# A spectral mixer with a token MLP on one core: a fixed engine order in the front, fixed PSUM banks and halved end units in the middle

## The chip, the cores and the metric

One NeuronCore of a Trainium2 chip runs the whole program. Its engines are TensorE (PE, with weight loads shown apart as PEld), VectorE (DVE), ScalarE (ACT), GpSimd (POOL) and SyncE (SP), which issues most of the DMAs. They run side by side, each takes its own instructions in the order in which they were written, and they wait for one another by semaphores. The metric is the time of one execution on the device, in microseconds (us).

## The reference

Two blocks, one after the other, on a sequence of 2048 tokens of 512 values, in bf16:

```python
def _A_ref(x, w_r, w_i):                 # x: 1 x 2048 x 512
    X = rfft2(x.astype(float32))         # over tokens and values: 2048 x 257 complex
    X = X * (w_r + 1j * w_i)             # one complex weight per frequency
    return irfft2(X, s=(S, D)).astype(bfloat16)

def _B_ref(x, w1, b1, w2, b2):           # mixes tokens: S = 2048, F = 1376
    h = _layernorm(x)
    u = gelu(einsum("bsd,sf->bdf", h, w1) + b1)
    return (einsum("bdf,fs->bds", u, w2) + b2).transpose(0, 2, 1)

h  = x + _A_ref(_layernorm(x), A_w_r, A_w_i)
h2 = h + _B_ref(_layernorm(h), B_w1, B_b1, B_w2, B_b2)
```

## The kernel before

The tokens are split as 128 partitions times 16 (n2), so x is sixteen tiles of 128 x 512. The Fourier transforms are written as matrix products with constant cosine and sine matrices, in five small stages, and the MLP as two large products.

1. **Front.** For each tile n2 the mean and the variance are found, on VectorE with `bn_stats` and `bn_aggr` (named st and ag, L653 and L654) or, for the tiles in `STAT_ACT`, on ScalarE with two passes and accumulators (s1, s2, L638) and two tiny steps on GpSimd (nm, bv). ScalarE turns the variance into 1/sigma (rs, L643 and L655; tiles of one entry of `RS_GROUPS` share one instruction). The 1/sigma of a tile scales its slice of the first Fourier matrix FP into FS (fs, on the engine that `FS_ENG` names, GpSimd otherwise). PE multiplies FS with the tile (f1: four matmuls of 256 columns per tile) into PSUM, and ScalarE, or VectorE for those in `Y_DVE`, copies the result to Y. One PSUM bank holds two tiles of one half b; there are sixteen copies of 512 elements.
2. **f2 and x.** The second transform works on Y of all sixteen tiles: for each of 16 values of G, four matmuls (f2), a copy to CS (cs; ScalarE, and VectorE for G = 1), and eight small matmuls (x) that fill two PSUM banks for two G's. Two G's make a unit u; there are eight.
3. **The multiply V (L739).** VectorE multiplies the PSUM of a unit with the filter weights W: one instruction of 2048 elements per unit, or two of 1024 where the unit is in `V_SPLIT`, here the first and the last.
4. **g1, g2, g3, the inverse transform.** g1 (16 matmuls per unit) is copied to PQ by ScalarE (pq, 512 elements for half a unit). g2 needs PQ of all units; its results are copied to EO, and g3 gives the filter block's output tile by tile. VectorE adds x (TT, H), ScalarE and VectorE normalise again (HH).
5. **The MLP.** 176 matmuls with W1 (mm1), gelu on ScalarE into GT, 176 with W2 (mm2), the last addition on VectorE, and the stores.

Nothing of this order is written out by hand. The class `Builder` collects the operations with their dependences, and `schedule` (L281) places them one at a time: of all operations that are ready it takes the one with the earliest planned start and, among equal starts, the one with the highest priority (`prio`), then the lowest index. The planned start uses a cost for each operation (`occ`: how long the engine is taken; `lat`: when the result is there) and a model of the DMA rate. The order in which operations are placed is the order of the instructions of each engine. PSUM units (`PsumUnit`) get banks at that moment: the bank, or neighbouring pair, that is free the earliest, with a limit on open units per class (f1 6, f2 2, x 2, g1 2).

At the start PE runs twenty matmuls on a tile of zeros (`warm`, L620 to L625; priority 50, while f1 has 14), which begin when VectorE's memset of that tile is done, and later some more behind the f1 matmuls (`WARM_AFTER`, priority 13) and ahead of the last half unit of g1 (`G1_WARM`).

The loads: x comes in six pieces and the FP constants in four; two of FP are issued by ScalarE, all else by SP. The filter weights W come in three pieces of units (0, 1 to 3, 4 to 7). A piece takes four DMAs for each of the two weight tensors, and the first piece six, because the row of partition `4 * (k2 * 2 + s) + 2 * sign + comp` (L37) interleaves the two signs of the frequency.

Of the kernel before, what the change touches and what calls it, by code (L numbers as in the profile page):

```python
# [6 lines left out]
ACT = mybir.ActivationFunctionType  # L7
# [29 lines left out]
def _row(sign, comp, k2, s):  # L37
    return 4 * (k2 * 2 + s) + 2 * sign + comp
# [52 lines left out]
def build_consts():  # L91
# [22 lines left out]
    fp = fp.reshape(NP, NS2, NP)  # L114
    fp = np.stack([-fp, fp], axis=2)
# [26 lines left out]
    c["E"] = e.reshape(NP, 1024)  # L142
    c["MR"] = np.concatenate([m.reshape(NP, 512), r.reshape(NP, 512)], axis=1)
# [5 lines left out]
PSUM_BANKS = 8  # L149
CELL = 4  # L150
# [28 lines left out]
class Builder:  # L179
    def __init__(self, nc, limits):  # L180
        self.nc = nc
        self.ops = []
        self.writer = {}
        self.readers = {}
        self.tensors = {}
        self.limits = limits
        self.cell_cache = {}

# [37 lines left out]
    def op(self, name, engine, emit, ins=(), outs=(), occ=100.0, lat=None, unit=None, pr=False, pw=False,  # L226
           first=False, last=False, prio=0, nbytes=0, is_dma=False, not_before=0.0, after=(), group=None, rate=DMA_RATE):
# [13 lines left out]
        o.rate = rate  # L241
        deps = {id(d): d for d in after}
# [38 lines left out]
    def schedule(self):  # L281
# [13 lines left out]
        order = []  # L295
        while len(order) < len(ops):
            best = None
            for o in ready:
                bank, avail = None, 0.0
                u = o.unit  # L300
                if u is not None and not u.claimed:
# [5 lines left out]
                    for b in range(PSUM_BANKS - u.nbanks + 1):  # L307
                        if all(bank_unit[i] is None for i in range(b, b + u.nbanks)):
# [13 lines left out]
            ready.remove(o)  # L322
            o.sched, o.start = True, st
# [11 lines left out]
            if o.is_dma:  # L335
                x0 = max(st + (3200.0 if st < 4000.0 else 1700.0), dma_free)
                dma_free = x0 + o.bytes / o.rate
# [89 lines left out]
def memory_layout():  # L427
# [26 lines left out]
    add("W", [NP, NG, 2, LW], bf, rw)  # L454
    add("HH", [NP, NS2, D_LEN], bf, rw)
# [28 lines left out]
STAT_ACT = (1, 3)  # L484
RS_GROUPS = ((0,), (2,), (4,), (5,), (6, 7), (8, 9), (10, 11), (12,), (13,), (14,), (15,))
FS_ENG = {4: "act", 7: "act", 9: "dve", 11: "dve", 13: "dve", 14: "act", 15: "dve"}
Y_DVE = ((5, 1), (6, 1), (7, 1))
N_WARM = 20
WARM_AFTER = (4, 3, 2, 1, 1, 0, 1, 0, 0, 0, 0, 0, 0, 0, 0, 0)
V_SPLIT = (0, 7)  # L490
# [4 lines left out]
def build_kernel(nc, A_x, A_w_r, A_w_i, B_w1, B_b1, B_w2, B_b2, out):  # L495
# [5 lines left out]
    K = Builder(nc, {"f1": 6, "f2": 2, "x": 2, "g1": 2, "g2": 2, "g3": 2, "mm1": 5, "mm1b": 6, "mm2": 8})  # L501
# [3 lines left out]
    X, FS, Y, CS, V, PQ, EO, H, HH, GT, OUT, W = (T[n] for n in ("X", "FS", "Y", "CS", "V", "PQ", "EO", "H", "HH", "GT", "OUT", "W"))  # L505
# [9 lines left out]
    def dma(name, dst, src, nbytes, stream="sp", outs=(), ins=(), prio=0, strided=False, after=(), group=None, rate=DMA_RATE,  # L515
            not_before=0.0):
        def emit(eng, bank):
            if strided:
                with nc.allow_non_contiguous_dma(reason="small bias gather"):
# [3 lines left out]
                    rate=rate, occ=1000.0 if stream == "pool" else 640.0 if rate < DMA_RATE else 460.0, not_before=not_before)  # L523
# [10 lines left out]
    def act(name, dst, src, func, n, ins=(), outs=None, unit=None, prio=0, last=True, psum=True, bias=None, scale=None, accum=None):  # L534
# [15 lines left out]
        return K.op(name, "act", emit, ins=ii, outs=oo, occ=lat - 90.0, lat=lat + 50.0, unit=unit, pr=unit is not None,  # L550
# [13 lines left out]
    def ldf(q, pr_, stream="sp", nb=0.0):  # L564
        sl = slice(4 * q, 4 * q + 4)
        dma(f"ld_FP{q}", FP[:, sl, :, :], cin[f"FP{q}"][:, :, :, :], 1 << 18, outs=[FP[:, sl, :, :]], prio=pr_, stream=stream, not_before=nb)

    for q, (a, b) in enumerate(((0, 2), (2, 4), (4, 6), (6, 8), (8, 12))):
        ldx(a, b, 90 - q)
    ldf(2, 84)  # L570
    ldx(12, 16, 83)
    ldf(3, 82)
    ldf(0, 90, "act")
    act("table", T["tb"][:, 0:1], EPS[:, 0:1], ACT.Abs_reciprocal_sqrt, 1, ins=[EPS[:, 0:1]], prio=88)
    ldf(1, 87, "act", 1800.0)
    dma("ld_E", EM[:, 0:1024], cin["E"][:, :], 1 << 18, outs=[EM[:, 0:1024]], prio=44)
    dma("ld_MR", EM[:, 1024:2048], cin["MR"][:, :], 1 << 18, outs=[EM[:, 1024:2048]], prio=43)
    wload = {}
    for ch, (u0, u1) in enumerate(((0, 1), (1, 4), (4, 8))):
        g0, ng = 4 * u0, 4 * (u1 - u0)  # L580
        lst = []
        for w, dram in ((0, A_w_r), (1, A_w_i)):
            for comp in range(2):
                d = W[comp::4, g0:g0 + ng, w, :]
# [296 lines left out]
```

## Time and profile before

| | us |
|---|---|
| median of 8 runs (lowest, highest) | 134.12 (133.69, 134.67) |
| profiled execution | 133.8 |
| its span, first to last instruction | 132.3 |
| PE busy, of the span | 124.8 (94%) |
| VectorE busy | 69.3 (52%) |
| ScalarE busy | 63.3 (48%) |
| GpSimd busy | 12.4 (9%) |
| granted TensorE clock, mean | 0.996 |

Stages by the timeline: the front from 4.8 (first tile there) to 18.8 (last copy to Y); f2 and x until the first multiply at 21.4; the multiplies until 39.3; g1, PQ and g2 until 42.5; the H stage until about 68; the rest of the MLP to the end. In a row of the timeline the first number is the start, the second how long the group lasted, then come engine, line of the kernel, operation, output and inputs, how many there were, and in brackets how long the engine had been idle and who ended that. In the chain of waits each row is a stretch of the path that ended last.

### The profile page before, as it was taken

How to read it: one execution, taken by the hardware profiler on the slowest of the kernel's cores; microseconds unless marked ns; L12 is line 12 of the kernel's file. 1: busy time of each engine (PE TensorE's matmuls, PEld its weight loads, DVE VectorE, ACT ScalarE, POOL GpSimd, SP SyncE). 2: the span in 40 equal slices, each digit the busy share in tenths (PEclk: the TensorE clock that was granted, in tenths of full speed). 3: DMA queues.
4: the chain of work that ended last, by engine and by line, in shares of the span. 5: the costliest groups of instructions: out<-in, count | busy, mean ns of one | idle time of the engine just before them, and what ended most of it. 6: DMA issues, size and time to landing. Idle time of an engine off the chain costs nothing.

```text
span 132.3 us, 2023 instructions
## 1 busy us (share of the span) xinstructions
PE 124.8 (94%) x786; PEld 74.6 (56%) x786; DVE 69.3 (52%) x127; ACT 63.3 (48%) x146; POOL 12.4 (9%) x33
## 2 busy tenths in 40 slices
PE   6999989999987979999999999999999999999990
PEld 2436656788666736544434444456666666666660
DVE  0499867999981999999960000000242332423322
ACT  4579976978966999976689322222000000000000
POOL 0299920000300000000000000000000000000000
PEclk9999999999999999999999999999999999999998
DMA  4999699999999999992000000000112112111121
GB/s 118 336 405 363 149 260 275 300 301 284 406 423 424 414 402 413 416 297 71 0 0 0 0 0 0 5 0 0 40 40 73 46 40 82 42 59 60 40 79 40
DMA packets 16648, 22.16 MB, mean 168 GB/s; under 512 B 2720, under 2 KB 12960, under 8 KB 16128
## 3 DMA queue, kind: packets, MB, share of 16 engines
q1 hardware_dynamic: 16352, 21.52, 47.6%
q10 hardware_dynamic: 288, 0.52, 1.3%
q8 instruction: 6, 0.10, 0.3%
q14 instruction: 2, 0.02, 0.0%
HBM read 19.95 MB, written 2.10 MB: 167 GB/s over the span
## 4 chain that ended last, share of the span: by engine, by line
PE 51%; DVE 32%; ACT 9%; DMA 3%; POOL 2%; issue 1%; DVEq 0%; ACTq 0%
PE ps L531 51%; DVE V L739 13%; DVE H L799 7%; ACT Y L549 5%; DVE TT L790 4%; DVE TT L792 4%; DVE HH L804 4%; DMA X<-in_A_x_dram 3%; POOL FS L633 1%; ACT rs L549 1%; ACT FS L549 1%; ACT JK L549 1%; DVE OUT L829 1%; PE ps L621 0%; ACT PQ L549 0%
## 5 line engine op out<-in xcount | busy, mean ns | idle before, releaser
L531 PE MATMUL ps<-HH,W 128*128 128x512 bf16 (+1 forms) x176 | 40.7, 379 | 1.2 <-DVE HH L804 0.9
L531 PE MATMUL ps<-GT,W 128*128 128x512 bf16 (+1 forms) x176 | 38.2, 379 | 0.0
L829 DVE SCALAR_TENSOR_TENSOR OUT<-ps,B2f,H 128x512 bf16<-128x512 f32 x16 | 12.0, 751 | 48.7 <-PE ps L531 48.7
L531 PEld LDWEIGHTS ps<-GT,W 128*128 128x128 bf16 (+1 forms) x176 | 25.3, 144 | 12.8
L531 PEld LDWEIGHTS ps<-HH,W 128*128 128x128 bf16 (+1 forms) x176 | 17.2, 100 | 21.3 <-DVE HH L804 1.9
L739 DVE TENSOR_TENSOR V<-ps,W 128x2048 bf16<-128x2048 f32 (+1 forms) x10 | 17.9, 1856 | 0.9 <-PE ps L531 0.9
L549 ACT ACTIVATE GT<-ps,B1f 128x512 bf16<-128x512 f32 (+1 forms) x11 | 7.1, 688 | 14.6 <-PE ps L531 14.6
L549 ACT ACTIVATE JK<-H,nm 128x512 bf16<-128x512 bf16 x16 | 11.6, 724 | 3.0 <-DVE H L799 2.9
L621 PE MATMUL ps<-ZT 128*128 128x512 bf16 x34 | 10.4, 445 | 1.3 <-DVE ZT L617 1.2
L653 DVE BATCH_NORM_STATS2 st<-X 128x6 f32<-128x512 bf16 x14 | 9.3, 671 | 4.0 <-DMA X<-in_A_x_dram 4.0
L799 DVE TENSOR_TENSOR H<-ps,TT 128x512 bf16<-128x512 f32 x16 | 11.0, 687 | 0.0
L549 ACT ACTIVATE PQ<-ps 128x512 bf16<-128x512 f32 x16 | 8.9, 603 | 3.5 <-PE ps L531 3.3
L549 ACT ACTIVATE EO<-ps 128x512 bf16<-128x512 f32 x16 | 9.2, 598 | 0.9 <-PE ps L531 0.9
L531 PE MATMUL ps<-EM,V 128*128 128x128 bf16 x128 | 9.2, 220 | 0.5 <-DVE V L739 0.5
L531 PE MATMUL ps<-EM,PQ 128*128 128x256 bf16 x64 | 9.0, 273 | 0.7 <-ACT PQ L549 0.7
L549 ACT ACTIVATE CS<-ps 128x512 bf16<-128x512 f32 x15 | 8.3, 608 | 2.1 <-PE ps L531 2.1
L531 PE MATMUL ps<-EM,Y 128*128 128x256 bf16 x64 | 8.7, 273 | 0.4 <-ACT Y L549 0.4
L531 PEld LDWEIGHTS ps<-EM,V 128*128 128x128 bf16 x128 | 7.5, 98 | 2.3 <-issue 1.4
L633 POOL TENSOR_SCALAR FS<-FP,rs 128x256 bf16<-128x256 bf16 x9 | 8.6, 962 | 0.6 <-ACT rs L549 0.5
L531 PE MATMUL ps<-FS,X 128*128 128x256 bf16 x64 | 8.4, 274 | 0.1
L790 DVE TENSOR_TENSOR TT<-ps,X 128x256 f32<-128x256 f32 x16 | 6.7, 421 | 3.3 <-PE ps L531 3.3
L531 PEld LDWEIGHTS ps<-EM,PQ 128*128 128x128 bf16 x64 | 6.2, 98 | 2.9 <-ACT PQ L549 0.9
(36 smaller groups left out, 79.7 us busy)
## 6 DMA issues: line engine op xcount, KB each, us to landing
W<-in_B_w_dram SPq DMA_DIRECT2D x4, 1376.0 KB, 12.0
W<-in_B_w_dram SPq DMA_DIRECT2D x10, 512.0 KB, 17.6
out_dram<-OUT SPq DMA_DIRECT2D x16, 128.0 KB, 1.7
W<-in_A_w_r_dram SPq DMA_DIRECT2D x4, 257.0 KB, 4.6
W<-in_A_w_i_dram SPq DMA_DIRECT2D x4, 257.0 KB, 4.7
X<-in_A_x_dram SPq DMA_DIRECT2D x4, 256.0 KB, 5.0
X<-in_A_x_dram SPq DMA_DIRECT2D x2, 512.0 KB, 6.7
W<-in_A_w_r_dram SPq DMA_DIRECT2D x4, 192.8 KB, 3.3
```

Of the source, the lines that this page charges most:

```text
L531: return K.op(name, "pe", lambda eng, bank: eng.matmul(outf(bank), lhsT, rhs, start=start, stop=stop), ins=ins or [lhsT, rhs], occ=occ, la ...
L549: return eng.activation(dst, s, func, **kw)
L621: return K.op(name, "pe", lambda eng, bank: eng.matmul(ps[:, bank, :], ZT[:, 0:NP], ZT[:, :], start=True, stop=True), ins=[ZT[:, :]], occ= ...
L633: dve(f"fs{i}", lambda eng, bank: eng.tensor_scalar(FS[:, i, :, :], FP[:, i, :, :], rs, None, op0=ALU.mult), [FP[:, i, :, :], rs], [FS[:, ...
L653: dve(f"st_{i}", lambda eng, bank, i=i, x=x: eng.bn_stats(ST[:, i, 0:6], x), [x], [ST[:, i, 0:6]], 512, prio=25)
L739: return eng.tensor_tensor(vout, s, win, ALU.mult)
L790: dve(f"tl_{s2}", lambda eng, bank, tt=tt, xl=xl: eng.tensor_tensor(tt[:, 0, :], ps[:, bank, 256:512], xl, ALU.add), [xl], [tt[:, 0, :]], ...
L792: dve(f"th_{s2}", lambda eng, bank, tt=tt, xh=xh: eng.tensor_tensor(tt[:, 1, :], xh, ps[:, bank, 256:512], ALU.subtract), [xh], [tt[:, 1, ...
L799: return eng.tensor_tensor(hs.rearrange("p (h d) -> p h d", h=2), e, tt[:, :, :], ALU.add)
L804: dve(f"hh_{s2}", lambda eng, bank, s2=s2, hs=hs: eng.tensor_scalar(HH[:, s2, :], hs, NM[:, s2:s2 + 1], R2[:, s2:s2 + 1], op0=ALU.add, op1 ...
L829: dve(f"fin{s2}", lambda eng, bank, dst=dst, bia=bia, hs=hs: eng.scalar_tensor_tensor(dst, ps[:, bank, :], bia, hs, op0=ALU.add, op1=ALU.add),
```

## The change

- The order of the front's operations is given by lists for VectorE, ScalarE, GpSimd and PE (`FRONT`). `schedule` takes an operation that is in a list only when all before it in the same list have been placed. Operations that are in no list, the fillers for example, are placed as before.
- The statistics of tiles 3 and 7 (before: 1 and 3) are found by ScalarE, from sums instead of means, so that one tiny GpSimd step (bv) lies on the way; nm moves behind the front. The FP slices of these tiles are scaled by 512 for it. The groups of rs and the engines of fs and of the copies to Y change. f1 fills a bank with one tile, both halves, or two neighbouring banks with two tiles; a copy to Y takes 512, 1024 or 256 elements, and VectorE does more of them.
- The first X piece of two tiles becomes two. ScalarE's two FP loads wait for the memset of zeros. Two loads of constants (E, MR) become one.
- The filter's rows are reordered (sign and comp swap) and the first filter piece gets a tile of its own, W0, weight tensor outermost, with eight DMAs instead of twelve.
- f2 and g1 use PSUM banks 0 to 3 only, x the pairs 4-5 and 6-7. f1 may have seven units open.
- Unit 0: each G's f2 result is copied in two halves, one by ScalarE, one by VectorE; each G's x has a unit of its own; the multiply is four instructions of 512 elements. Only unit 7 stays in `V_SPLIT`.
- The last half unit of g1 takes two banks, and its copy to PQ is two of 256 elements, the first by VectorE, the second by ScalarE.
- In the planner's costs a ScalarE operation takes the engine 30 ns less, and a DMA starts 1750 ns after its issue at 340 bytes/ns at first.

```diff
-    return 4 * (k2 * 2 + s) + 2 * sign + comp
+    return 4 * (k2 * 2 + s) + 2 * comp + sign
...
+    for i in STAT_ACT:
+        fp[:, i] *= D_LEN
...
+CLASS_BANKS = {"x": (4, 6), "f2": (0, 1, 2, 3), "g1": (0, 1, 2, 3)}
...
+        pos = {n: (e, i) for e, lst in self.forced.items() for i, n in enumerate(lst)}
+        done = {e: 0 for e in self.forced}
         while len(order) < len(ops):
             best = None
             for o in ready:
+                if o.name in pos and done[pos[o.name][0]] != pos[o.name][1]:
+                    continue
...
-                        if all(bank_unit[i] is None for i in range(b, b + u.nbanks)):
+                        if b in CLASS_BANKS.get(u.cls, range(8)) and all(bank_unit[i] is None for i in range(b, b + u.nbanks)):
...
-STAT_ACT = (1, 3)
-RS_GROUPS = ((0,), (2,), (4,), (5,), (6, 7), (8, 9), (10, 11), (12,), (13,), (14,), (15,))
-FS_ENG = {4: "act", 7: "act", 9: "dve", 11: "dve", 13: "dve", 14: "act", 15: "dve"}
-Y_DVE = ((5, 1), (6, 1), (7, 1))
+STAT_ACT = (3, 7)
+RS_GROUPS = ((0,), (1,), (2,), (4,), (5, 6), (8, 9), (10, 11), (12,), (13,), (14, 15))
+FS_ENG = {0: 'dve', 6: 'act', 7: 'act', 9: 'act', 10: 'dve', 15: 'dve'}
+Y_EVAC = (('single', ('dve',), ('act',)), ('pair', 'act'), ('pair', 'act'), ('pair', 'act'), ('single', ('act',), ('dve',)), ('pair', 'dve'), ('single', ('act',), ('act',)), ('single', ('dve', 'act'), ('act',)))
+FRONT = {
+    "dve": """bn_0 ag_0 fs_0 bn_1 ag_1 ys_0 bn_2 bn_4 ag_4 ag_2 bn_5 bn_6 ag_5 ag_6 bn_8 bn_9 ag_8 bn_10 ag_9 bn_13 ag_10
+        ag_13 bn_11 ag_11 bn_12 fs_10 ag_12 bn_14 bn_15 ag_14 ag_15 ys_9 fs_15 yp_5 yh_140""",
+    "act": """rs_0 rs_1 s1_3 s2_3 rs_3 ys_1 rs_2 rs_4 s1_7 rs_5 s2_7 fs_6 yp_1 rs_8 rs_7 fs_9 rs_13 fs_7 rs_10 yp_2 rs_12
+        yp_3 rs_14 ys_8 ys_13 ys_12 ys_15 yh_141""",
+    "pool": """fs_1 bv_3 fs_3 fs_2 fs_4 bv_7 fs_5 fs_8 fs_13 fs_11 fs_12 fs_14""",
+    "pe": """f1_0 f1_1 f1_3 f1_2 f1_4 f1_6 f1_5 f1_9 f1_8 f1_7 f1_10 f1_11 f1_13 f1_12 f1_15 f1_14""",
+}
-V_SPLIT = (0, 7)
+V_SPLIT = (7,)
...
     def stage_f2(u):
         for i in range(2):
             G = 2 * u + i
-            unit = PsumUnit("f2", 1)
+            split = u == 0
...
+                if split:
+                    dst = CS[:, G, par, :, :].rearrange("p c j -> p (c j)")
+                    src = lambda bank, par=par: ps[:, bank, par * 256:par * 256 + 256]
+                    if par == 0:
+                        a_ = act(f"cs_{G}_0", dst, src, ACT.Copy, 256, unit=unit, prio=14)
+                    else:
+                        d_ = dve(f"cs_{G}_1", lambda eng, bank, dst=dst, src=src: eng.tensor_copy(dst, src(bank)), [], [dst], 256, unit=unit, prio=14)
+                        cs_ops[G] = [a_, d_]
...
     def stage_x(u):
...
+            if u == 0:
+                for w in range(2):
+                    wt = W0[:, w, i::2, :]
+                    win = bass.AP(wt.tensor, wt.offset + 1, [list(wt.ap[0]), [2 * LW, 2], [1, 2], [2, NP]])
+                    vout = V[:, i:4:2, w, :].rearrange("p g (y j) -> p g y j", y=2)
...
+                    K.op(f"v_0_{i}{w}", "dve", tw, ins=[wt], outs=[vout], occ=598.0, lat=720.0, unit=unit, pr=True, last=w == 1, prio=11, after=wload[0])
...
     def stage_g1(u):
...
+            split = (u, h) == (7, 1)
...
+                    if gi == 1:
+                        act(f"pq_{u}_{h}{gi}", dst, src, ACT.Copy, 256, unit=unit, prio=15)
+                    else:
+                        dve(f"pq_{u}_{h}{gi}", lambda eng, bank, dst=dst, src=src: eng.tensor_copy(dst, src(bank)), [], [dst], 256, unit=unit, prio=15)
```

In the new names bn is `bn_stats` (st before), and ys, yp and yh are the copies to Y of one tile, of a pair of tiles and of half a tile.

## The prediction

> **What bounds the kernel now.** I read the page first (shares by engine, the 40 slices), then the chain that ended last, then the timeline engine by engine for the first 45 us, then the busy times by stage. Times are us from the start of the span.
>
> The chain gives the order of the bounds. It runs through ScalarE and PE until 21.4, through VectorE's ten multiplies until 39.3, over a short handover to 42.5, through VectorE again to 67.9, and PE to the end:
>
> ```profile
> 17.01 1.47 ACT Y L549 x3
> 18.48 0.05 issue
> 18.53 2.77 PE ps L531 x25
> ...
> 21.39 1.04 DVE V L739
> 22.43 0.10 issue
> 22.53 15.62 DVE V L739 x8
> ...
> 40.04 0.61 ACT PQ L549
> 40.65 0.05 issue
> 40.70 1.82 PE ps L531 x14
> ...
> 67.97 61.15 PE ps L531 x282
> ```
>
> From 40.70 on PE has almost no holes: 352 matmuls of 512 columns at 0.216, 64 of 256 at 0.109 and 16 more of 512 are 86.4 us of issue in the 88.4 until 129.11. So the time is "when does g2 start" (40.70) plus something that this change does not touch, and the sum can be made at three marks: the last piece of Y (18.84), the first multiply (21.39), g2's first matmul (40.70).
>
> The front ends at the first mark. VectorE's rows show the step that matters here, statistics at a steady 0.66 per tile and a last eviction ending at 18.15+0.69:
>
> ```profile
> 7.43 0.66 DVE L653 BATCH_NORM_STATS2 st<-X 128x6 f32<-128x512 bf16 x1
> 8.00 0.17 DVE L654 BATCH_NORM_AGGREGATE mv<-st 128x2 f32<-128x6 f32 x1
> 8.08 0.66 DVE L653 BATCH_NORM_STATS2 st<-X 128x6 f32<-128x512 bf16 x1
> ...
> 18.15 0.69 DVE L692 CAST Y<-ps 128x512 bf16<-128x512 f32 x1 [0.29 <-PE ps L531]
> 19.77 0.69 DVE L712 CAST CS<-ps 128x512 bf16<-128x512 f32 x1 [0.92 <-PE ps L531]
> ```
>
> By 8.08 four tiles have had their statistics; ten remain. PE's rows show what occupies it before the front's first matmul:
>
> ```profile
> 1.17 6.32 PE L621 MATMUL ps<-ZT 128*128 128x512 bf16 x20 [1.17 <-DVE ZT L617]
> 7.44 0.61 PE L531 MATMUL ps<-FS,X 128*128 128x256 bf16 x4
> ```
>
> Twenty filler matmuls hold PE until 7.3 (the last one starts about 7.11, which is 7.49 minus the 0.38 of one; 0.216 apart by then).
>
> **The change, part by part.**
>
> *Front order (the large term).* The lists fix each engine's order. VectorE's begins bn_0 ag_0 fs_0 bn_1 ag_1 ys_0 bn_2. ys_0 evicts f1_0. The twenty fillers stay: they have priority 50, f1 has 14, and the planner picks the earliest start and then the higher priority, so a ready f1_0 ties with the next filler and loses, twenty times. f1_0 can therefore not begin before 7.11+0.22 = 7.33, however early tile 0 lands; its four matmuls (0.11 apart, the last 0.27 long) end at 7.93, and ys_0 starts at 7.98. VectorE has nothing left before it: with tile 0 down by 3.6 to 4.8 and the first FP piece by about 5.0 (before: issued 0.71, 3.9 to 4.5 to land; now behind the memset, 0.45 later), ag_1 is over by 6.2. It stands about 1.8 us with twelve tiles' statistics queued behind it, where the kernel before had ten left at 8.08.
>
> From 7.98, by VectorE's own rows: ys_0 0.61; twelve bn+ag at 0.66 = 7.92; five places where an ag follows its own bn (0.73 instead of 0.57 after its start, or part of it) 0.5; fs_10 and fs_15 0.19 each; ys_9 0.61; yp_5 of 1024 elements 1.13 (the pitch of the 1024-element multiply); yh_140 0.42. Sum 11.57: 19.55.
>
> ScalarE: ag_2 ends at 10.1, so rs_2 starts there; then in list order with rs 0.19, s1 or s2 0.63, fs 0.40, Y of 512 0.485 (0.97 for two in the chain), Y of 1024 0.91 (0.485 plus another 512 at the 0.83 ns per element that 512 and 256 elements differ by): it waits for ag_6 (11.55), reaches yp_1 at 12.8, yp_2 at 15.2, yp_3 at 16.3, waits for ag_15 until 17.3, then rs_14, four ys and yh_141: 19.8. GpSimd: fs_2 from 10.55, then fs_4, bv_7, fs_5 to 13.6, fs_8 from 14.05 (rs_8 waits for ag_9), then four more at 0.93: fs_14 ends at 18.7, f1_14 at 19.4. So all three end between 19.4 and 19.8, which is tight: any handover that slips is paid. Before, VectorE lost 1.5 us between 8.08 and 18.84 to waits (10.76 minus 9.27 of work); I have counted 0.5 for it. Between nothing more and 0.9 more I take 0.35, nearer the lower end because the largest waits are already in. Last Y: 20.15 against 18.84, **+1.3**.
>
> What the front gives away is hidden: ScalarE's Y work falls from 13 x 0.485 = 6.3 to 5.4, but it now waits for VectorE.
>
> *First units in halves.* Before, from the last Y (18.84) to the first multiply (21.39) is 2.55: four f2 matmuls, one 0.6 and one 0.69 eviction that both had to be done (20.46), eight x matmuls, the multiply. Now x of G=0 alone needs cs_0 in two halves: f2 half done 0.3 after the last Y, ScalarE's half 0.40, VectorE's half 0.42 (the 128x256 row) starting 0.22 later, so both at +1.0; 0.18 to the first x matmul as before; four instead of eight (0.16+0.27); 0.14 to the multiply: 1.75. Between 1.6 and 2.05 (if the halves cost as much as wholes). **-0.8.** It comes off whatever the front does.
>
> *Unit 0 in four multiplies of 512.* No such row; between two 256s (0.33 pitch each) and half a 1024 (0.565): the H row of 512 from PSUM has a pitch of 0.60. 4 x 0.61 = 2.44 against 2 x 1.13. **+0.18**; 0 to +0.4. The next multiply needs banks 4 and 5, free after the second small one (1.2 us earlier) and 0.7 of x: ready before VectorE is. g1 of unit 0 now needs all four pieces; f2 of later units fills PE.
>
> *Last unit in halves.* From the last multiply's end (39.33) to g2 (40.70): g1 0.07, eight matmuls to 40.01, a 0.61 eviction. Now the first 256 goes to an idle VectorE, the second to ScalarE at 0.40: **-0.2**; 0 to -0.3.
>
> *Banks 0 to 3 for f2 and g1, 4 to 7 for x.* The same two x pairs that the limit allowed. The eight x units fed VectorE without a hole (16.90 busy of 16.90), so no gain; if a bank made x late, each 0.1 is paid in full. 0, with 0 to +0.4.
>
> *Transfers.* SP: one X issue more (0.46), one constant fewer (0.45), first W piece 8 instead of 12 at 0.65: later issues go out 2.6 us earlier. No multiply waited for W, and none does when the first starts at about 21.9; 0. FP from ScalarE's queue 0.45 later: hidden under the fillers until 7.33, a cover of 2 us. The two moved-off nm steps leave GpSimd 0.2 each earlier; it waits for rs anyway. The planner's ScalarE step is 30 ns shorter, which may reorder the later stages: 0, with -0.3 to +0.3.
>
> The rule that bears on the thinner PE stream is in the Trainium skill, "TensorE: Matmul & The Clock Gate", Part 1: after an idle window of about 3.4 us the array falls to half rate. The rows of before show only the start of it (weights 0.43 apart for nine fillers, then 0.22) and no later gap to judge by. By it my longest hole in the new front, some 1.3 us before f1_2, costs nothing; a half-rate f2 and x would be an estimated 0.9 more.
>
> **Sum**: 1.3 - 0.8 + 0.18 - 0.2 = +0.48. The profiled execution took 133.8 (span 132.3 plus 1.5 around it), 0.3 under the median 134.12; +0.48 on 133.8 is 134.3, on the median **134.6**.
>
> **Rivals.**
> - *No stall (faster).* If f1_0 starts ahead of the fillers' end, at 5.3 to 5.6 when fs_0 is done, ys_0 costs no wait. bn_2 starts at 6.6 or so instead of 8.6, everything above ends 1.9 earlier (GpSimd's ten fs from 6.5 then set 17.9), and the sum is -1.75: 132.4. For it: the list reads as if PE were free. Against: the twenty fillers and the priorities are unchanged. It decides wherever f1_0 starts before about 6.9: each 0.1 earlier is worth 0.1, and 0.9 undoes the loss and passes the bound below.
> - *The stall without the extra slips (no change).* Last Y at 19.8: +0.13, 134.25. For it: all three chains were worked out with their waits. Against: 1.5 of waits in the front of before.
> - *Multiplies starve (much slower).* If the x units come late in the middle because g1 of unit 0 is put off by 1.4 us onto a PE that has 16.2 of 16.9 filled, VectorE gets holes; one PE turn (0.6 to 1.0) is the likely price: 135.5. For it: PE's and VectorE's work per unit are nearly equal (8 f2 at 0.109, 8 x at 0.054 and 16 g1 at 0.056 are 2.20 against 2.23). Against: f2 can run ahead.
>
> **How the numbers follow.** Stall with slips 0.50, no change 0.20, no stall 0.17, starving 0.13. A difference under 0.3% (0.4 us) can't be told from none. The likeliest case alone spans 133.9 to 135.2: it gives 0.31 slower, 0.13 same, 0.06 faster. No change gives 0.14 same, 0.03 each side; no stall is faster, starving slower but for 0.01. Faster 0.26, same 0.28, slower 0.46. For 8 in 10: 133.0 leaves most of the no-stall case out (0.14), 135.3 half of the starving one (0.06).
>
> **What would show it.** PE: fillers x20 and then f1 at 7.3 to 7.5. VectorE: an idle of 1.5 to 2 us before a cast to Y near 8.0, the next statistics at 8.6, the last cast of 256 ending near 20. First multiply near 21.9, four of about 0.7, then six of 2.28 without a hole; last end to g2 1.15. Wrong if f1_0 or the second tile's statistics start well before these, or if the multiplies show idle time.

## The result, and the profile after

The changed kernel takes 135.81 us (median of 11 runs, 135.09 to 136.46); the kernel before takes 134.23 (median of 31, 133.69 to 134.84). The ratio is 1.0119, with a 95% interval of 1.0100 to 1.0139. The direction is the one forecast, the size is not: +1.58 on the medians where +0.48 was predicted, and 135.81 lies above the range that was given (133.0 to 135.3). Here and below a median is over all executions of a kernel, while a ratio with its interval leaves out executions more than 1.5% above the kernel's fastest, which are 2 of 10 with ten fillers, 3 of 10 with ten fillers and the old step, and 1 of 7 in the last run.

The profiled execution of the kernel after took 136.29 (span 134.4), that of before 133.8 (span 132.3). These two differ by 2.49, more than the medians do: the one of after is near the top of its runs and the one of before near the bottom. Why is shown below. Times are again us from the start of the span.

I read the marks that the prediction used. First VectorE's timeline of the kernel after (start, length, engine, line, operation and tiles; in brackets the idle time before and what ended it):

```profile
3.18 0.69 DVE L679 BATCH_NORM_STATS2 st<-X 128x6 f32<-128x512 bf16 x1 [2.07 <-DMA X<-in_A_x_dram]
...
4.66 0.69 DVE L679 BATCH_NORM_STATS2 st<-X 128x6 f32<-128x512 bf16 x1
...
8.87 0.69 DVE L737 CAST Y<-ps 128x512 bf16<-128x512 f32 x1 [3.31 <-PE ps L552]
9.48 1.28 DVE L679 BATCH_NORM_STATS2 st<-X 128x6 f32<-128x512 bf16 x2
...
19.06 1.54 DVE L737 CAST Y<-ps 128x1024 bf16<-128x1024 f32 x2
...
22.57 2.48 DVE L806 TENSOR_TENSOR V<-ps,W 128x512 bf16<-128x512 f32 x4 [0.32 <-PE ps L552]
25.29 15.88 DVE L821 TENSOR_TENSOR V<-ps,W 128x2048 bf16<-128x2048 f32 x8 [0.23 <-PE ps L552]
```

This is the stall that the prediction described, and longer than described: VectorE has two tiles' statistics by 5.6, then stands 3.31 before the first copy to Y, which starts at 8.87 and not at 7.98; the third tile's statistics follow at 9.48. Of the 1.5 by which the stall is longer, 0.9 is the later start of the copy and 0.6 that the second tile's statistics are done earlier (5.6 and not 6.2). Of the multiplies, four of 512 take 2.48, and there is idle time (0.23) where the prediction expected none. In the profile of before the ten multiplies are one row:

```profile
21.39 17.88 DVE L739 TENSOR_TENSOR V<-ps,W 128x1024 bf16<-128x1024 f32 x10 [0.93 <-PE ps L531]
```

What VectorE waits for ahead of the first copy to Y stands in PE's timeline:

```profile
1.17 7.23 PE L645 MATMUL ps<-ZT 128*128 128x512 bf16 x20 [1.17 <-DVE ZT L590]
8.24 1.04 PE L552 MATMUL ps<-FS,X 128*128 128x256 bf16 x8
```

The twenty fillers last 7.23 here; in the profile of before they last 6.32. The chain of waits gives the new order of the bounds:

```profile
1.17 7.23 PE ps L645 x20
8.40 0.45 PE ps L552 x4
8.87 0.69 DVE Y L737
9.57 1.20 DVE st L679 x2
...
18.50 2.23 ACT Y L570 x5
20.75 13.51 PE ps L552 x163
34.28 4.50 DVE V L821 x2
...
46.43 0.81 ACT JK L570 x2
...
70.36 61.15 PE ps L552 x282
```

Three things are new against before: the fillers begin the chain and set the front; from 20.75 to 34.26 it runs through PE and not through the multiplies; and behind g2 it runs through ScalarE until 57.6, where before it went through VectorE from 42.54 on. From 70.36 on the 282 matmuls are the 61.15 of before.

The marks, run by run, each from the timelines of one profiled execution. "f1" is the first f1 matmul, "last Y" the end of the last copy to Y, "multiplies" from the start of the first to the end of the last, "g2" its first matmul, "PE end" the end of its last matmul.

| run | f1 | last Y | first multiply | multiplies | g2 | g2 to PE end | PE end | profiled time | median |
|---|---|---|---|---|---|---|---|---|---|
| before | 7.44 | 18.84 | 21.39 | 17.88 | 40.70 | 88.42 | 129.12 | 133.8 | 134.23 |
| after | 8.24 | 20.72 | 22.57 | 18.60 | 42.45 | 89.06 | 131.51 | 136.29 | 135.81 |
| ys_0 later | 7.56 | 19.51 | 21.27 | 18.60 | 41.16 | 89.04 | 130.20 | 134.91 | 134.47 |
| ten fillers | 5.11 | 18.21 | 19.97 | 18.60 | 39.85 | 89.04 | 128.89 | 133.6 | 134.53 |
| middle alone | 7.91 | 18.96 | 20.63 | 18.51 | 40.43 | 88.41 | 128.84 | 133.56 | 133.39 |
| middle alone, free banks | 7.33 | 18.73 | 20.41 | 18.86 | 40.48 | 88.42 | 128.90 | 133.78 | 133.79 |
| front alone | 8.20 | 20.67 | 23.41 | 17.80 | 42.63 | 89.05 | 131.68 | 136.37 | 135.95 |
| old ScalarE step | 7.04 | 19.51 | 21.37 | 18.51 | 41.17 | 88.41 | 129.58 | 134.57 | 135.04 |
| old loads, ys_0 later | 7.25 | 19.14 | 20.91 | 18.60 | 40.79 | 89.04 | 129.83 | 134.86 | 134.65 |
| old loads and step, ys_0 later | 7.97 | 19.27 | 21.03 | 18.52 | 40.84 | 88.41 | 129.25 | 134.32 | 134.30 |
| 24 fillers | 8.19 | 20.67 | 22.52 | 18.60 | 42.41 | 89.04 | 131.45 | 136.2 | 136.67 |
| 16 fillers | 5.94 | 18.42 | 20.27 | 18.60 | 40.15 | 89.05 | 129.20 | 133.93 | 135.35 |
| ten fillers, old step | 5.41 | 18.28 | 20.05 | 18.51 | 39.85 | 88.41 | 128.26 | 133.16 | 133.99 |
| four fillers, old step | 4.81 | 19.15 | 20.91 | 18.52 | 40.72 | 88.40 | 129.12 | 133.94 | 133.82 |
| ten fillers, old step, none later | 5.19 | 19.39 | 21.15 | 19.76 | 42.20 | 88.92 | 131.12 | 135.98 | 135.81 |

After minus before at the end of PE's work is 2.39: the front +1.88, the handover to the first multiply -0.70 (2.55 to 1.85), the multiplies +0.72, the handover to g2 -0.15, and the part behind g2 +0.64. On the medians the same terms leave an estimated +1.07 for the front: 1.58 less the other four, which sum to +0.51.

### The profile page after: what moved, and what is told of

It reads as the page before. It is cut to its first block, busy times and chain, and to the rows that moved or that the text cites. A ratio compares the mean times of both kernels' runs of the same rounds, so it can differ in the third digit from the quotient of the medians.

```text
span 134.4 us, 2025 instructions
## 1 busy us (share of the span) xinstructions
PE 126.5 (94%) x786; PEld 74.7 (56%) x786; DVE 71.5 (53%) x131; ACT 62.5 (47%) x142; POOL 12.8 (9%) x33
## 4 chain that ended last, share of the span: by engine, by line
PE 65%; DVE 16%; ACT 14%; issue 3%; ACTq 0%
PE ps L552 59%; PE ps L645 6%; ACT JK L570 4%; DVE H L896 4%; ACT Y L570 3%; DVE V L821 3%; ACT EO L570 3%; DVE HH L901 2%; DVE st L679 2%; DVE TT L887 2%; DVE TT L889 2%; ACT r L570 1%; ACT rs L570 1%; ACT FS L570 1%; ACT PQ L570 1%
## 5 line engine op out<-in xcount | busy, mean ns | idle before, releaser
L821 DVE TENSOR_TENSOR V<-ps,W 128x2048 bf16<-128x2048 f32 (+1 forms) x8 | 15.7, 2018 | 0.4 <-PE ps L552 0.2
L645 PE MATMUL ps<-ZT 128*128 128x512 bf16 x34 | 11.2, 477 | 1.4 <-DVE ZT L590 1.2
L570 ACT ACTIVATE PQ<-ps 128x512 bf16<-128x512 f32 (+1 forms) x16 | 9.1, 590 | 3.7 <-PE ps L552 3.6
L657 POOL TENSOR_SCALAR FS<-FP,rs 128x256 bf16<-128x256 bf16 x10 | 9.2, 927 | 8.1 <-ACT rs L570 8.1
L570 ACT ACTIVATE CS<-ps 128x512 bf16<-128x512 f32 (+1 forms) x16 | 8.4, 575 | 1.6 <-PE ps L552 1.6
L645 PEld LDWEIGHTS ps<-ZT 128*128 128x128 bf16 x34 | 3.9, 119 | 6.9 <-issue 3.6
```

The lines of the kernel that those rows point to most:

```text
L570: return eng.activation(dst, s, func, **kw)
L645: return K.op(name, "pe", lambda eng, bank: eng.matmul(ps[:, bank, :], ZT[:, 0:NP], ZT[:, :], start=True, stop=True), ins=[ZT[:, :]], occ= ...
L657: dve(f"fs_{i}", lambda eng, bank: eng.tensor_scalar(FS[:, i, :, :], FP[:, i, :, :], rs, None, op0=ALU.mult), [FP[:, i, :, :], rs], [FS[:, ...
L821: return eng.tensor_tensor(vout, s, win, ALU.mult)
```

## The experiments

**Which half of the change costs what.** Two kernels split it. The first takes before and adds everything in the middle: row order, W0 and its loads, banks, the pieces of unit 0 and of the last half unit. Its front, its X and FP loads and its planner's costs are those of before.

```diff
-    return 4 * (k2 * 2 + s) + 2 * sign + comp
+    return 4 * (k2 * 2 + s) + 2 * comp + sign
...
+CLASS_BANKS = {"x": (4, 6), "f2": (0, 1, 2, 3), "g1": (0, 1, 2, 3)}
...
-V_SPLIT = (0, 7)
+V_SPLIT = (7,)
...
+            split = u == 0
...
+            split = (u, h) == (7, 1)
```

> The kernel before with only the middle of the change (row order and W0, fixed banks, unit 0 in halves and four multiplies, the last half unit in two banks); the front, its loads and the planner's costs stay. Queue theory: nothing is lost here. From the trace of the changed kernel: head -0.7, unit 0 +0.45, the other multiplies +0.2, tail -0.1, so 133.9 to 134.3. Rival (the middle costs): 135.0 or more.

Measured: 133.39, ratio 0.9941 (0.9914 to 0.9969). It beats both kernels and its own forecast. The marks are plain: the front as before (18.96), from the last Y to the first multiply 1.67 and not 2.55, the multiplies 18.51 and not 17.88, from the last multiply to g2 1.29 and not 1.43, and behind g2 88.41 as before. By the trace the three changed terms sum to -0.39 (-0.88, +0.63, -0.14), which is at the edge of the interval.

The second does the reverse: the kernel after, with the middle of before.

```diff
-    return 4 * (k2 * 2 + s) + 2 * comp + sign
+    return 4 * (k2 * 2 + s) + 2 * sign + comp
...
-CLASS_BANKS = {"x": (4, 6), "f2": (0, 1, 2, 3), "g1": (0, 1, 2, 3)}
+CLASS_BANKS = {}
...
-V_SPLIT = (7,)
+V_SPLIT = (0, 7)
...
-            split = u == 0
...
-            split = (u, h) == (7, 1)
```

> The changed kernel with the middle of the kernel before (its row order, W loads, free banks, f2, x, multiplies and g1); front, lists, X and FP loads and planner's costs of the change stay. Queue theory: the last Y at 20.7 as in the changed kernel, so +1.9 on the kernel before and no gain behind it: 135.8 to 136.3. Rival (the middle costs): 134.0 to 134.5.

Measured: 135.95, ratio 1.0125 (1.0082 to 1.0168). The whole loss is in the front lists, the loads and the planner's costs; and 0.63 of it arises behind g2 (89.05), where no line of the kernel was changed.

**Is it the place of ys_0?** The copy of f1_0 moves behind three more tiles' statistics in VectorE's list; nothing else changes.

```diff
-    "dve": """bn_0 ag_0 fs_0 bn_1 ag_1 ys_0 bn_2 bn_4 ag_4 ag_2 bn_5 bn_6 ag_5 ag_6 ...
+    "dve": """bn_0 ag_0 fs_0 bn_1 ag_1 bn_2 bn_4 ag_4 ag_2 bn_5 ys_0 bn_6 ag_5 ag_6 ...
```

> The changed kernel with one word moved: ys_0, the first copy to Y, stands behind bn_5 in VectorE's list instead of ahead of bn_2. Queue theory (the fillers hold f1_0, ys_0 holds the twelve statistics behind it): VectorE's 3.3 us of idle before ys_0 shrinks to under 1, the second group of statistics starts when its tile lands (7.0) instead of 9.5, the last Y moves from 20.7 to 18.8 to 19.1, and the time falls by 1.6 to 1.9 us to 133.9 to 134.3. Rival that the middle is what costs (four small multiplies, fixed banks): the front has slack and the time stays at 135.4 or more.

Measured: 134.47 against 134.1 for before in the same runs, ratio 1.0026 (1.0005 to 1.0048). The time is a little above the forecast, and so is the last Y (19.51). So the wait at ys_0 is real, and most of the front's loss goes with it. VectorE's timeline of this run shows what is late next:

```profile
5.45 0.18 DVE L680 BATCH_NORM_AGGREGATE mv<-st 128x2 f32<-128x6 f32 x1
7.36 1.29 DVE L679 BATCH_NORM_STATS2 st<-X 128x6 f32<-128x512 bf16 x2 [1.74 <-DMA X<-in_A_x_dram]
```

The statistics of the third tile now wait for its load until 7.36. Before, the second group of statistics began at 6.06. With the first X piece cut in two, tile 0 is down earlier (statistics at 2.86 to 3.55 in the runs with the new loads, 4.52 to 4.86 in those with the old), but the piece behind comes later.

**Is it the fillers?** The list stays, and the number of fillers at PE's start changes: 10, 24 and 16 in place of 20.

```diff
-N_WARM = 20
+N_WARM = 10
```

> The changed kernel with ten fillers at the start instead of twenty, the lists untouched. Queue theory: f1_0 starts at about 5.5, ys_0 at about 6.5, before the next tiles have landed, so VectorE loses almost nothing to it and the time falls as with ys_0 moved, to 133.9 to 134.4, unless PE then runs its first matmuls at the slow spacing for longer, which is worth up to 0.4. Rival (the middle costs): 135.4 or more.

> The changed kernel with 24 fillers at the start instead of 20, the lists untouched. Queue theory: the last Y follows the first f1 matmul by 12.47 us as in the changed kernel and in the two others that keep its lists, so four fillers at 0.216 push everything back by 0.86: 136.4 to 136.9. Rival (fillers of zeros only fill idle time, and the front is bound by the statistics or the loads): 135.6 to 136.0, as with 20.

> The changed kernel with 16 fillers. Queue theory: 0.86 less than with 20, 134.7 to 135.2, and the same 12.47 from the first f1 matmul to the last Y, as long as the second pair of tiles (6.5 to 7.4) has not become the later of the two. Rival: 135.6 to 136.0.

Measured: 134.53 with ten (1.0014; 0.9993 to 1.0036), 136.67 with 24 (1.0213; 1.0158 to 1.0269), 135.35 with 16 (1.0079; 1.0047 to 1.0110). Four more cost 0.86 on the medians, which is four times 0.216, though over four executions and with an interval of some 0.75 to either side; four fewer give 0.46 and not the 0.86 that was expected. Both ends of the ten executions with 16 are lower by about as much as expected (133.93 and 135.57 against 135.09 and 136.46), but six of the ten stand near the upper one. PE's timelines, of the runs with 10, 24 and 16 in this order:

```profile
1.17 4.10 PE L645 MATMUL ps<-ZT 128*128 128x512 bf16 x10 [1.17 <-DVE ZT L590]
5.11 0.60 PE L552 MATMUL ps<-FS,X 128*128 128x256 bf16 x4
```

```profile
1.17 7.19 PE L645 MATMUL ps<-ZT 128*128 128x512 bf16 x24 [1.17 <-DVE ZT L590]
8.19 1.04 PE L552 MATMUL ps<-FS,X 128*128 128x256 bf16 x8
```

```profile
1.17 4.93 PE L645 MATMUL ps<-ZT 128*128 128x512 bf16 x16 [1.17 <-DVE ZT L590]
```

Twenty-four fillers in one execution end as early as twenty in another. What differs is how many of them run at half rate. In PE's timeline of weight loads they are 0.43 apart until 4.95 in the profile of before (nine slow), and until 6.69 in that of after (thirteen slow). These are of before:

```profile
4.56 0.15 PEld L621 LDWEIGHTS ps<-ZT 128*128 128x128 bf16 x1 [0.27 <-issue]
4.95 2.04 PEld L621 LDWEIGHTS ps<-ZT 128*128 128x128 bf16 x10 [0.23 <-issue]
```

and these of after:

```profile
6.27 0.15 PEld L645 LDWEIGHTS ps<-ZT 128*128 128x128 bf16 x1 [0.28 <-issue]
6.69 1.21 PEld L645 LDWEIGHTS ps<-ZT 128*128 128x128 bf16 x6 [0.28 <-issue]
```

In the profiles of this study twenty fillers lasted from 5.91 to 7.23, and the profile of after holds the longest: this fits its place near the top of its runs. Where ys_0 stands first in VectorE's list and waits for f1_0, that goes into the time one for one: last Y minus f1 is 12.48, 12.47, 12.47, 12.48 and 12.48 in the runs after, front alone, old ScalarE step, 24 fillers and 16 fillers. In the front of before it doesn't: middle alone has f1 0.47 later than before, and last Y only 0.12 later.

The Trainium skill has a rule for this, in "TensorE: Matmul & The Clock Gate", Part 1: the window that opens the clock runs freely, the transition comes where the first matmul happens to fall in it, and a cold count must not be fitted. This case agrees that it varies: the slow spacing ended between 3.7 and 6.7 with the start always at 1.17. These 3.0 lie within one of the page's windows of 3.4, and are wider than the half microsecond to either side that it gives for the transition. The page also says that the ramp costs under 1% of a typical span; here the spread of the fillers alone, 1.32, is about 1% of 134, because a queue stands behind them.

**What moved behind g2?** The kernel after, with the planner's ScalarE step as long as before.

```diff
-        return K.op(name, "act", emit, ins=ii, outs=oo, occ=lat - 120.0, lat=lat + 50.0, ...
+        return K.op(name, "act", emit, ins=ii, outs=oo, occ=lat - 90.0, lat=lat + 50.0, ...
```

> The changed kernel with one planner number restored: a ScalarE operation is planned 30 ns longer again (lat minus 90). PE's order behind g2 is then that of the kernel before's middle-only version. Order theory (the new cost reorders the H stage and loses 0.64 there): from g2's first matmul to PE's end 88.4 instead of 89.05, and 0.6 less in all, 135.1 to 135.4. Rival (the H stage is slower because it starts later, not because of its order): 89.0 again and 135.6 to 136.0.

Measured: 135.04, ratio 1.0073 (1.0047 to 1.0098), against 1.0119 for the kernel after; and g2 to the end of PE is 88.41, as before. So these 30 ns in a table of costs are worth 0.64 behind g2, where nothing but the order of instructions differs. The order of PE and ScalarE differs in the multiplies as well, and there the step is worth another 0.09: 18.60 with the new step and 18.51 or 18.52 with the old one, in each of three pairs of kernels (20 fillers, ten fillers, old loads). VectorE's timelines show where it shifts. After:

```profile
46.56 0.68 DVE L896 TENSOR_TENSOR H<-ps,TT 128x512 bf16<-128x512 f32 x1
47.16 0.41 DVE L889 TENSOR_TENSOR TT<-X,ps 128x256 f32<-128x256 bf16 x1
47.49 0.42 DVE L887 TENSOR_TENSOR TT<-ps,X 128x256 f32<-128x256 f32 x1
47.94 0.42 DVE L901 TENSOR_SCALAR HH<-H,nm,r 128x512 bf16<-128x512 bf16 x1
48.26 0.69 DVE L896 TENSOR_TENSOR H<-ps,TT 128x512 bf16<-128x512 f32 x1
```

ScalarE's r (1/sigma of the second normalisation) for the first HH is, after:

```profile
47.61 0.29 ACT L570 ACTIVATE r<-v,eps 128x1 f32<-128x1 f32 x1
```

VectorE with the old step:

```profile
46.54 0.68 DVE L896 TENSOR_TENSOR H<-ps,TT 128x512 bf16<-128x512 f32 x1
47.14 0.40 DVE L901 TENSOR_SCALAR HH<-H,nm,r 128x512 bf16<-128x512 bf16 x1
47.46 0.41 DVE L889 TENSOR_TENSOR TT<-X,ps 128x256 f32<-128x256 bf16 x1
```

After, the first HH stands ahead of the third H; it needs ScalarE's r, which ends at 47.90, so it starts 0.45 behind the TT before it, where 0.33 is usual: VectorE loses 0.12. With the old step three H go first, and HH at 47.14 finds its r done (it ends at 46.61). From there on VectorE and ScalarE wait for each other in turn, and the chain of after goes through ScalarE's JK (its pass over H for the variance), r and EO until 57.6; with the old step it stays on VectorE from 43.02.

**Are the new loads the next limit?** The run with ys_0 later gets the X pieces and the FP loads of before; and, in a second kernel, the old ScalarE step as well.

```diff
-    for q, (a, b) in enumerate(((0, 1), (1, 2), (2, 4), (4, 6), (6, 8), (8, 12))):
+    for q, (a, b) in enumerate(((0, 2), (2, 4), (4, 6), (6, 8), (8, 12))):
...
-    ldf(0, 92, "act", after=[zt])
-    ldf(1, 91, "act", after=[zt])
+    ldf(0, 100, "act")
+    ldf(1, 94, "act")
```

> The kernel with ys_0 moved (e1) and the X and FP loads of the kernel before (two tiles in the first piece, FP not waiting for the memset). Load theory (the finer first piece puts the second pair of tiles back from 6.1 to 7.0 to 7.4, and VectorE stands for it): the pair lands at 6.1 to 6.5, but tile 0 lands at 4.5 to 4.8 and its scaling goes first, so bn_2 begins at 7.0 to 7.1 instead of 7.36 and the time falls by 0.2 to 0.4, to 134.1 to 134.3. Rival (what is left of the front's loss is in the lists' handovers): 134.4 to 134.7.

> e6 with the planner's ScalarE cost restored as well: if both terms are separate they add, 0.6 under e6, 133.4 to 133.8; faster than the kernel before, and about as fast as the middle alone (133.4). If the order of the later stages depends on the front, anything up to 134.5.

Measured: 134.65 (1.0042; 1.0027 to 1.0057) and 134.30 (1.0003; 0.9986 to 1.0020). The load theory was missed: the loads of before bring nothing on the median against 134.47, and the time lies where the rival had it. The second misses 133.4 to 133.8 because the first does; the old step itself gives 0.5 by the two ratios, and g2 to the end of PE is 88.41 again. Last Y is 19.14 and 19.27 in these two; before ends at 18.84. Tile 0's statistics start at 4.86 and 4.69, as in before, but fs_0, next in VectorE's list, waits for ScalarE's rs_0 ahead of bn_1, so that bn_1 starts at 6.33 and 6.17 and the third tile's statistics only at 7.16 and 6.99 (before: 6.06). So, without the stall and without the new loads, the searched order is still no faster than the old one. What holds its end stands in the chain of waits of the first of the two:

```profile
8.67 0.61 PE ps L552 x4
9.28 1.08 PE ps L645 x5
...
15.66 2.83 PE ps L552 x22
```

From the second f1 group at 8.67 the chain stays on PE until 18.50, through f1 and eleven later fillers (2.57 of it); in before it ran through ScalarE there. Whether the front would end sooner without those fillers no run shows.

**Do the fixed banks do anything?** Middle alone, without the limits on the banks.

```diff
-CLASS_BANKS = {"x": (4, 6), "f2": (0, 1, 2, 3), "g1": (0, 1, 2, 3)}
+CLASS_BANKS = {}
```

> The middle alone (e3) without the fixed banks: f2, g1 and x take any bank again. If the banks are worth nothing, as predicted: 133.2 to 133.6, as the middle alone. Rival (the fixed banks carry the middle's gain, or cost something): a difference of 0.4 or more either way, seen as holes between the multiplies.

Measured: 133.79 (0.9970; 0.9950 to 0.9989). The multiplies take 18.86 and not 18.51, so by the trace the fixed banks, with the order of PE that the planner makes for them, are worth 0.35 within this middle; the medians differ by 0.40, and the two intervals overlap. VectorE's timeline of this run, then that of middle alone:

```profile
20.41 2.48 DVE L754 TENSOR_TENSOR V<-ps,W 128x512 bf16<-128x512 f32 x4 [0.33 <-PE ps L533]
23.02 4.49 DVE L769 TENSOR_TENSOR V<-ps,W 128x2048 bf16<-128x2048 f32 x2
27.69 11.58 DVE L769 TENSOR_TENSOR V<-ps,W 128x2048 bf16<-128x2048 f32 x6 [0.18 <-PE ps L533]
```

```profile
20.63 2.48 DVE L754 TENSOR_TENSOR V<-ps,W 128x512 bf16<-128x512 f32 x4 [0.32 <-PE ps L533]
23.35 8.88 DVE L769 TENSOR_TENSOR V<-ps,W 128x2048 bf16<-128x2048 f32 x4 [0.23 <-PE ps L533]
32.39 6.75 DVE L769 TENSOR_TENSOR V<-ps,W 128x2048 bf16<-128x2048 f32 x4 [0.17 <-PE ps L533]
```

Both have PE as what ended the waits. In middle alone the excess over before's 17.88 is 0.20 for four instructions of 512 (2.48 against two of 1024 at 1.14 each), 0.24 and 0.16 of waiting for x, and 0.03 besides.

**Fewer fillers and the old step together, and what fillers are good for.** The two mends of the front and of the order behind g2 in one kernel, with ten fillers; then with four.

```diff
-N_WARM = 20
+N_WARM = 10
...
-        return K.op(name, "act", emit, ins=ii, outs=oo, occ=lat - 120.0, lat=lat + 50.0, ...
+        return K.op(name, "act", emit, ins=ii, outs=oo, occ=lat - 90.0, lat=lat + 50.0, ...
```

> Ten fillers and the planner's old ScalarE cost, the lists untouched: the two terms that were found, both taken out. If they add: 0.6 under the ten fillers alone, 133.7 to 134.1 in the median and 133.0 at best, so faster than the kernel before by 0.1 to 0.4 and not faster than the middle alone (133.4). The ten fillers alone spread from 133.6 to 136.4; if short warming is the reason, this one spreads as far, and a slow execution shows the first f1 matmuls 0.21 apart instead of 0.11.

> The kernel after with 4 fillers instead of 20 at PE's start, and ScalarE's planned step 30 ns longer as before (that is, the run with ten fillers and the old step, with six fillers fewer). Open is why that run had three of its ten executions at 135.50 to 135.62 with a mean granted clock of 0.987 and the others at 133.16 to 134.16 with 0.997 or more: 1.3% of 134 is 1.7 us of lost clock, as if some 3.5 us ran at half rate. Theory A, the fillers only hold f1 back and the clock is not their doing: with f1 no longer held (it waits for its filter slice at about 5), nothing changes against ten fillers: 133.2 to 134.2, clock 0.997 or more in most executions, 0.987 in about a third as before. Theory B, the fillers also keep the rate up, and a front with little PE work in a window loses it: with four fillers most executions are at 0.987 or less and at 135.5 or more, and the profile shows, somewhere before 15 us, f1's matmuls of 256 columns 0.21 apart instead of 0.11 after they had been 0.11 apart, or the slow start lasting longer than 7.

Measured: 133.99 (0.9966; 0.9941 to 0.9990) with ten, 133.82 (0.9977; 0.9953 to 1.0000) with four. Both are level with the kernel before or a little below it, and neither is better than middle alone. With ten, three of the ten executions took 135.50 to 135.62 with a mean granted clock of 0.987; the other seven took 133.16 to 134.16 with 0.997 or more. (Of the run with ten fillers and the new step two of ten were like this, at 136.05 and 136.44.) With four there were none, where theory A had expected a third and theory B most; the times (133.18 to 134.26) are those of theory A, and the slow start that lasts longer is a mark of theory B. PE's timeline with four fillers:

```profile
1.17 1.89 PE L645 MATMUL ps<-ZT 128*128 128x512 bf16 x4 [1.17 <-DVE ZT L590]
4.81 1.03 PE L552 MATMUL ps<-FS,X 128*128 128x256 bf16 x4 [1.75 <-DVE FS L657]
5.90 1.89 PE L645 MATMUL ps<-ZT 128*128 128x512 bf16 x4
```

Four f1 matmuls take 1.03 where they take 0.60 otherwise, and the spacing becomes 0.22 for fillers only from 10.9 on. Last Y is at 19.15 with f1 at 4.81; with ten fillers it is at 18.28 with f1 at 5.41. So four fillers pay for an earlier f1 with a slower front.

The last kernel keeps ten fillers at the start and takes away those between the groups of f1.

```diff
-WARM_AFTER = (4, 3, 2, 1, 1, 0, 1, 0, 0, 0, 0, 0, 0, 0, 0, 0)
+WARM_AFTER = (0,) * 16
```

> The run with ten fillers and the old ScalarE step, without the fillers between the front's f1 groups (all counts in the list of later fillers 0; ten at the start stay). Theory C: the start's rate, once up, falls for one window where the front's PE stream is thin; then most executions show a mean granted clock of about 0.987 and 135 to 136, and the profile shows f1 or f2 matmuls of 256 columns 0.21 apart for some 3.5 after they had been 0.11 apart. Theory D: the executions at 135.5 have another cause than the thin stream; then the shares stay as with ten fillers (about a quarter at 0.987, the rest 133.2 to 134.2), and if the later fillers themselves stand in f1's way, the rest is up to 0.4 faster.

Measured: 135.81 (1.0108; 1.0067 to 1.0149). All seven executions had a granted clock of 0.975 to 0.987. The busy times by stretch show the drop (from:to, length, busy time and count of PE, weight loads, VectorE, ScalarE and GpSimd, then granted clock, DMA share, GB/s):

```profile
4.00:8.00 4.00, 2.40 (x12) 1.00 (x10) 3.09 (x7) 1.73 (x6) 1.25 (x2) 1.00 1.02 340
8.00:10.00 2.00, 0.62 (x4) 0.43 (x4) 2.00 (x7) 2.00 (x8) 1.61 (x2) 0.59 1.03 380
10.00:12.00 2.00, 2.00 (x10) 1.02 (x9) 2.00 (x7) 1.59 (x4) 2.00 (x4) 0.50 1.02 403
12.00:14.00 2.00, 2.00 (x12) 1.43 (x10) 1.68 (x7) 1.95 (x8) 1.66 (x3) 0.50 1.06 355
14.00:16.00 2.00, 2.00 (x15) 1.56 (x14) 2.00 (x7) 1.22 (x3) 2.00 (x3) 0.70 1.17 304
```

PE's timeline has its longest hole there:

```profile
9.38 6.87 PE L552 MATMUL ps<-FS,X 128*128 128x256 bf16 x35 [1.90 <-POOL FS L657]
```

From the shares, the rate was half from about 8.4 to about 15.2: 6.8 at half rate, which over a span of 134.1 makes the mean of 0.975 that this execution has; 0.987 is half as long. The first multiply is at 21.15, 1.10 later than with the later fillers in place. G2 is at 42.20, 2.35 later, but the other 1.25, which arise in the multiplies (19.76), and the 88.92 behind g2 can't be put down to the rate: the granted clock is 1.00 from 16 on, and without the fillers the planner makes another order of PE from about 19 on. For the rate theory C holds: a thin stream of matmuls in the front loses it, and the fillers between the groups of f1 hold it, in 15 of 20 executions with ten fillers at the start. That the other five, at 0.987, are the same thing fits in time and clock; none of them was seen in a trace, so it is argued and not shown.

## Why the prediction was wrong, step by step

Two terms of the sum failed. The planner's shorter ScalarE step, put at 0, measured +0.64 behind g2; and unit 0 in four, put at +0.18 because x would be "ready before VectorE is", measured +0.72 over the multiplies. The front, the large term, came near its size by the estimate from the medians (+1.07 against +1.3).

**The front order: the mechanism was right.** f1_0 begins behind the twenty fillers, ys_0 waits for it, and the rest of VectorE's list waits behind ys_0. From f1's start on the three chains were worked out to 19.80 minus 7.33, 12.47; five runs have 12.47 or 12.48. Marks on the way agree too, so this is not luck: in after ScalarE starts the three copies of pairs at 13.68, 16.17 and 17.26, where 12.8, 15.2 and 16.3 were worked out, each 0.9 to 1.0 earlier, as is f1 itself (7.33 against 8.24). The 0.35 for further slips was not there; it was taken from 1.5 of waits in the front of before, where the profile has VectorE busy for 9.82 of the 10.76, so idle for 0.94. What the prediction missed here is in "f1_0 can therefore not begin before 7.33", used as if it were a time: 7.33 is where the fillers ended in one execution. In the profile of after f1 begins at 8.24. By the profiles the front is +1.88 and not +1.31. Since both fillers and time vary from execution to execution, the medians leave about +1.07, so for the median the front was not the term that missed.

**The first units in halves, -0.8**, measured -0.70 in after and -0.88 in middle alone. Right, and it did come off whatever the front did.

**Unit 0 in four, +0.18**, measured +0.72 for the multiplies as a whole. The price of the pieces was right (2.48 against 2.28, +0.20). Wrong was "ready before VectorE is": VectorE waits 0.24 for x behind the fourth small piece (25.05 to 25.29). PE had no hole there, but thirteen matmuls of f2, most of them for later units, stood ahead of the eight of x:

```profile
23.02 1.59 PE L552 MATMUL ps<-EM,Y 128*128 128x256 bf16 x13
24.54 0.61 PE L552 MATMUL ps<-CS,EM 64*128 64x256 bf16 x8
```

The remaining 0.28 is two short waits further on: the multiplies at 31.89 and 34.28 start 2.39 apart and those at 36.49 and 38.81 2.32, where 2.20 is usual; in middle alone one wait of 0.16 takes their place, and the difference of 0.09 goes with the planner's step. The chain of after runs through PE from 20.75 to 34.26. That is the third rival's outcome, x late on a PE with nearly as much work per unit as VectorE, though ahead of the first late x stood f2 running ahead, which the prediction had counted against this rival, and not a put-off g1. I gave it 0.13 and priced it at one PE turn of 0.6 to 1.0, and it came at 0.52, beside the stall and not in place of it.

**The banks, 0 with 0 to +0.4.** As part of the new middle, with the order that goes with them, they give 0.35; the bounds excluded a gain, on the ground that VectorE had no hole in before. It had none with the old unit 0; the new one opens holes, and the banks close part of them.

**The last unit in halves, -0.2**, measured -0.15. **Transfers, 0**: no multiply waited for W. In the front the claim was less good: with ys_0 out of the way the third tile's load is the next wait, to 7.36.

**The planner's 30 ns, 0 with -0.3 to +0.3.** Measured +0.64, the largest miss of the sum. The prediction treated a change of the planner's costs as noise of either sign with a bound that stood on no row; the stage behind g2 is one where VectorE had 0.10 of idle in 25.43, so a new order there had next to nothing to win and could lose a good deal; in after 0.38 of 26.06 are idle. "Something that this change does not touch", said of all behind g2, was wrong for the same reason.

**The sum.** Predicted 134.6, measured 135.81: +1.21. Behind g2 it is 0.64, in the multiplies 0.54, in the two handovers 0.10 and 0.05, and 0.11 is that the median of before is 134.23 over all runs and not 134.12; the front takes back 0.24. The cases were also set up as rivals of which one would happen, while the front's stall, half of the starving and the new order all came together. With the upper ends of the single terms in one sum the range would have held the time.

**The rule of the skill.** The prediction said, by "TensorE: Matmul & The Clock Gate", Part 1, that holes of some 1.3 without PE work cost nothing since it takes an idle window of about 3.4. In after the rate did hold (granted clock 1.00). The reading of the rule, one hole against one window, did not: in the last experiment PE's longest hole was 1.90 (7.48 to 9.38) and the rate fell inside it, at about 8.4. What measure the chip goes by the runs don't show; PE was busy for 2.40 of the 4.00 between 4 and 8 there. The stretch at half rate, 6.8, is two of the page's windows.

## What to carry to other kernels

An instruction that waits in a list holds all that is listed behind it, and it carries the spread of what it waits for into the time: ask not only when its input comes, but how much that varies between executions, and put work that needs nothing ahead of it. When a planner's cost is changed, however little, compare the order that comes out in every stage, above all in one where an engine has no idle time to give. Two gains in a change that loses are worth taking out: the middle alone is 0.6% faster than before (0.3 to 0.9).

## What the runs showed of the hardware

- The start of PE at half rate is not of fixed length: with the first matmul always at 1.17, the slow spacing (0.43 for 512 columns) ended between 3.7 and 6.7 with ten or more fillers, and at 10.9 with four fillers in a front with holes.
- The granted clock of the profile reads 1.00 in that time: with four fillers every stretch from 0 to 14 has 1.00 although f1 matmuls of 256 columns are about 0.21 apart until 10.6 (0.11 behind that). A drop later on is shown (0.59, 0.50, 0.50, 0.70). For the start, go by the spacing of the weight loads.
- With the first X load cut in two (and ScalarE's FP loads issued later, which no run separates) the first half lands some 1.0 to 2.0 earlier (statistics at 2.86 to 3.55 against 4.52 to 4.86). What comes behind is later for it: where VectorE was free to take it, the next group of statistics began at 6.55 to 7.36 (ten fillers, four fillers, ys_0 later) and not at 6.06 to 6.38 (before, middle alone, free banks).
